# Moving all 128x128 transposes of an attention and MLP layer from TensorE to crossbar DMAs

## The chip, the cores and the metric

One core of a Trainium2 chip. The metric is the device time of one execution in microseconds (us). Runs of one kernel agree within about 0.7%. Engine names: PE is TensorE, PEld its weight load, DVE is VectorE, ACT is ScalarE, POOL is GpSimd, SP is SyncE. "SPq" and "ACTq" rows are DMA issues on the two rings.

## The reference

Tokens S = 2048, width D = 1024, 32 query heads of 32 with one shared K and V head, MLP width F = 3584, all bf16.

```python
h  = x + A(layernorm(x))        # A: q = x wq (32 heads), k = x wk, v = x wv,
                                #    softmax(q k^T / sqrt(32)) v, then wo
h2 = h + B(layernorm(h))        # B: (sigmoid(x w_gate) * (x w_up)) w_down
```

A matmul here contracts over the partitions, so three intermediates have to be transposed in 128x128 blocks: the normalised x (16 tiles of 128x1024), the attention output (16 tiles) and the normalised h (16 tiles).

## The kernel before

A planner in Python simulates the five engines with assumed durations and emits one fixed, in-order instruction list for each engine. Semaphores keep the result correct whatever the real times are. The order is the planner's guess.

Names used below: `xT` transposes the normalised x; `KV` makes K and V; `Q0` and `Q` make the queries; `S` is a block of scores, followed by two exponentials `Pr` on ACT; `PV` is the product with V; `OTt` transposes the attention output; `OP` is the output projection; `hT` transposes the second norm's result; `GU(c)` is the gate and up product of token chunk c (256 tokens, 28 groups); `D(c)` is the down product. GU(0) needs the attention of query tiles 0 and 1 (128 exponentials), their OP, the second norm and hT.

```python
# the planner's model of one DMA (all DMAs are on the SP ring)
if o.nbytes:
    go = max(s + 1300.0, self.dma_free)
    self.dma_free = go + o.nbytes / 260.0
    o.end = self.dma_free + 700.0
...
PRIO = ["xT", "KV", "Q0", "PV", "OTt", "OP", "hT", "D", "GU", "Q"]   # who fills TensorE first
...
def mk_xT(t):                                   # head: 8 TensorE transposes, one PSUM copy
    def atoms(b):
        tp = F_ps[:, b, :].bitcast(BF16)
        return [(lambda dt=dt: PE.transpose(out=tp[:, dt * P:(dt + 1) * P],
                 in_=xn[:, t % 2, dt * P:(dt + 1) * P], identity=ident[:, :]), P, []) for dt in range(DT)]
    def after(b, last):
        ...                                     # ACT or DVE copies PSUM to xnT, then the next norm is queued
...
def mk_OTt(hh):                                 # attention output: 4 transposes, DVE copy to OT (32 groups)
def mk_hT(t):                                   # second norm: 8 transposes, DVE copy to hnT (16 groups)
...
# when the last Q group is done: w_down, 7.3 MB in four pieces, into the memory of xnT and wq
for i in range(4):
    wd_ld.append(dma(lambda ...: SP.dma_start(wd_sb[:, a:b2, :], ...), f"wd{i}", 7 * P * D * 2, [last], prio=4))
```

All matmul groups except S share two PSUM banks (F_ps). A bank is free again when its copy has been made.

The softmax here doesn't subtract the row's maximum and nothing guards it: scores larger than these inputs give would overflow.

## Time and profile before

| | before |
|---|---|
| median time | 1221.6 us (3 runs; 1223.2 with the fourth, taken beside the change) |
| TensorE busy / ACT busy | 1174.0 / 1042.1 of 1223.8 us |
| first K/V matmul | 13.75 us |
| first exponential | 27.3 us |
| first GU(0) matmul | 177.7 us |

From the page of the kernel before: the busy times, then the rows of the 40 slices (digits are tenths of a slice of 30.6 us; PEclk is the granted TensorE clock in tenths).

```profile
PE 1174.0 (96%) x22016; PEld 835.1 (68%) x22016; DVE 316.4 (26%) x838; ACT 1042.1 (85%) x1283; POOL 47.2 (4%) x109
PE   4899979999999999999999999999999999999999
ACT  6899999999999999999999999999999989711120
PEclk9999989999999999999999999999999999999999
DMA  9411175562056601565016460256303653089390
```

TensorE and ACT are both full from the third slice on. The exponentials end near 1062 us, and the last 160 us are bound by TensorE. So TensorE work that disappears from the middle, or an idle TensorE that is filled, shortens the tail. The dip to 8 in slice 6 is a stretch where TensorE has too little to do.

The table of stretches, TensorE only: from:to, length, busy us (instructions), granted clock, DMA share, GB/s.

```profile
0.00:60.00 60.00, 38.86 (x705) 1.00 0.72 222
60.00:150.00 90.00, 89.32 (x1806) 1.00 0.13 38
150.00:210.00 60.00, 50.74 (x1132) 0.91 0.61 199
210.00:265.00 55.00, 54.56 (x1164) 1.00 0.58 157
265.00:1060.00 795.00, 780.97 (x15952) 1.00 0.39 109
```

TensorE idles 21.1 us in the first 60, 9.3 us in the stretch around 180 us, and 14.0 us in the long middle. Between 150 and 210 us the Q groups have been used up and GU(0) may not start yet: the attention alone, paced by ACT, leaves TensorE partly empty.

The TensorE timeline at two places in the middle, with start, length, and in brackets the idle time before with its releaser. First an OTt group, then the two hT groups of a chunk:

```profile
678.18 0.76 PE L330 MATMUL F_ps<-hnT,ring 128*128 128x256 bf16 x3
678.78 0.39 PE L558 MATMUL F_ps<-ident,Osb 128*128 128x128 bf16 x4
679.68 0.60 PE L330 MATMUL F_ps<-wo_sb,OT 128*128 128x512 bf16 x2 [0.52 <-DVE OT L566]
...
1019.93 0.61 PE L619 MATMUL F_ps<-ident,hn 128*128 128x128 bf16 x8
1020.47 0.40 PE L330 MATMUL S_ps<-QTb,kT 32*128 32x128 bf16 x16
1021.33 0.62 PE L619 MATMUL F_ps<-ident,hn 128*128 128x128 bf16 x8 [0.45 <-DVE hnT L625]
1021.78 1.03 PE L330 MATMUL F_ps<-zone,hact 128*128 128x512 bf16 x4
```

Four transposes stream in 0.23 us (eight start within 0.62 us, which is 57 ns each), but from the start of the OTt group to the next instruction 0.90 us pass, because the next group waits for the copy.

### The profile page before, as it was taken

The numbers are of one execution on the slowest core, as the hardware profiler recorded it, in microseconds if no ns is written. First come the engines' busy times: TensorE is split into PE (matmuls) and PEld (weight loads), VectorE is DVE, ScalarE is ACT, GpSimd is POOL, SyncE is SP. The second block draws the span as 40 slices with busy tenths as digits, with TensorE's granted clock in tenths as the row PEclk, the third lists the DMA queues.
The fourth block names the chain that finished last, engine by engine and source line by source line (L and its number), as shares of the span: only waits on it lengthen the run. The fifth ranks groups of instructions, "written<-read, shape, count | busy, mean of one in ns | idle before, by whom it ended". The sixth has DMA issues, their size and how long they took to land.

```text
span 1223.8 us, 47137 instructions
## 1 busy us (share of the span) xinstructions
PE 1174.0 (96%) x22016; PEld 835.1 (68%) x22016; DVE 316.4 (26%) x838; ACT 1042.1 (85%) x1283; POOL 47.2 (4%) x109
## 2 busy tenths in 40 slices
PE   4899979999999999999999999999999999999999
PEld 3665557785678756877568675778657776587684
DVE  8523321212222222223121222132222212232121
ACT  6899999999999999999999999999999989711120
POOL 6100000000000000000000000000000000000000
PEclk9999989999999999999999999999999999999999
DMA  9411175562056601565016460256303653089390
GB/s 320 116 28 41 42 260 156 148 173 64 20 149 174 192 20 46 150 191 148 16 50 191 119 170 20 70 165 184 111 20 86 172 148 102 15 224 263 105 252 18
DMA packets 258612, 151.02 MB, mean 123 GB/s; under 512 B 7280, under 2 KB 248944, under 8 KB 258416
## 3 DMA queue, kind: packets, MB, share of 16 engines
q1 hardware_dynamic: 258416, 148.00, 43.1%
q8 instruction: 173, 2.83, 1.0%
q14 instruction: 23, 0.19, 0.0%
HBM read 140.64 MB, written 7.34 MB: 121 GB/s over the span
## 4 chain that ended last, share of the span: by engine, by line
PE 63%; ACT 31%; issue 3%; DVE 2%; POOL 0%; DMA 0%
PE F_ps L330 54%; ACT Pr L495 28%; PE S_ps L330 9%; ACT tnh L669 1%; ACT zone L313 1%; PE F_ps L619 0%; ACT zone L230 0%; DVE OT L566 0%; DVE st L274 0%; DVE st L276 0%; PE F_ps L558 0%; DMA ring<-in_A_x_dram 0%; POOL dsb L287 0%; DVE hnT L625 0%; DVE ring L307 0%
## 5 line engine op out<-in xcount | busy, mean ns | idle before, releaser
L495 ACT ACTIVATE Pr<-S_ps 128x1024 bf16<-128x1024 f32 x1024 | 972.4, 1052 | 26.4 <-PE S_ps L330 25.9
L330 PE MATMUL F_ps<-hnT,ring 128*128 128x256 bf16 x3584 | 440.6, 275 | 2.5 <-DVE OT L566 1.2
L330 PEld LDWEIGHTS F_ps<-hnT,ring 128*128 128x128 bf16 x3584 | 332.5, 98 | 61.3 <-issue 3.1
L330 PEld LDWEIGHTS F_ps<-Vaug,Pr 128*128 128x128 bf16 x8192 | 229.7, 96 | 28.1 <-issue 4.1
L330 PE MATMUL F_ps<-Vaug,Pr 128*128 128x33 bf16 x8192 | 244.4, 178 | 2.4 <-issue 1.5
L330 PE MATMUL S_ps<-QTb,kT 32*128 32x128 bf16 x8192 | 208.5, 218 | 15.4 <-ACT Pr L495 10.1
L330 PE MATMUL F_ps<-zone,hact 128*128 128x512 bf16 x896 | 213.2, 380 | 0.8 <-DVE OT L566 0.5
L330 PEld LDWEIGHTS S_ps<-QTb,kT 32*128 32x128 bf16 x8192 | 119.2, 93 | 127.9 <-ACT Pr L495 81.6
L676 DVE SCALAR_TENSOR_TENSOR hact<-tnh,F_ps 128x256 bf16<-128x256 f32 x224 | 94.3, 421 | 384.0 <-ACT tnh L669 383.9
L669 ACT ACTIVATE tnh<-F_ps 128x256 f32<-128x256 f32 x224 | 90.7, 405 | 115.0 <-PE F_ps L330 115.0
L330 PEld LDWEIGHTS F_ps<-zone,hact 128*128 128x128 bf16 x896 | 79.2, 98 | 91.3 <-DVE OT L566 0.7
L330 PE MATMUL F_ps<-zone 128*128 128x256 bf16 (+2 forms) x512 | 76.5, 292 | 3.1 <-POOL rstd L290 1.2
L707 DVE SCALAR_TENSOR_TENSOR h_sb<-F_ps,h_sb 128x512 bf16<-128x512 f32 x32 | 22.1, 692 | 203.1 <-PE F_ps L330 203.1
L330 PE MATMUL F_ps<-wo_sb,OT 128*128 128x512 bf16 x256 | 64.2, 381 | 3.8 <-DVE OT L566 3.7
L531 DVE RECIPROCAL rL<-F_ps 128x4 f32<-128x4 f32 x128 | 23.4, 183 | 133.7 <-PE F_ps L330 133.5
L330 PEld LDWEIGHTS F_ps<-zone 128*128 128x128 bf16 x512 | 37.5, 98 | 24.2 <-ACT zone L230 1.4
L284 POOL TENSOR_SCALAR zb<-mvb 128x1 bf16<-128x1 bf16 x32 | 7.5, 233 | 1026.4 <-DVE mvb L280 1026.1
L330 PEld LDWEIGHTS F_ps<-wo_sb,OT 128*128 128x128 bf16 x256 | 21.0, 97 | 28.4 <-DVE OT L566 6.9
L533 DVE TENSOR_TENSOR Osb<-F_ps,rL 128x128 bf16<-128x128 f32 x128 | 37.2, 291 | 3.8
L594 DVE TENSOR_TENSOR h_sb<-F_ps,xres 128x512 bf16<-128x512 f32 x32 | 22.1, 692 | 54.4 <-PE F_ps L330 54.4
L337 PE MATMUL F_ps<-ident,zone 128*128 128x128 bf16 x128 | 11.0, 236 | 17.3 <-POOL dsb L287 9.1
L231 DVE CAST hact<-F_ps 128x512 bf16<-128x512 f32 x24 | 16.6, 692 | 40.2 <-PE F_ps L330 40.2
(39 smaller groups left out, 232.4 us busy)
## 6 DMA issues: line engine op xcount, KB each, us to landing
ring<-in_B_w_gate_dram SPq DMA_DIRECT2D x112, 512.0 KB, 4.1
ring<-in_B_w_up_dram SPq DMA_DIRECT2D x112, 512.0 KB, 5.9
zone<-in_B_w_down_dram SPq DMA_DIRECT2D x4, 1792.0 KB, 15.4
ring<-in_A_x_dram SPq DMA_DIRECT2D x16, 256.0 KB, 7.0
xres<-in_A_x_dram SPq DMA_DIRECT2D x16, 256.0 KB, 2.7
out_dram<-h_sb SPq DMA_DIRECT2D x32, 128.0 KB, 1.7
q_scratch<-hact SPq DMA_DIRECT2D x24, 128.0 KB, 1.8
QTb<-q_scratch SPq DMA_DIRECT2D x6, 512.0 KB, 6.3
```

What stands on the lines that cost most here:

```text
L231: lambda: DVE.tensor_copy(out=out_ap, in_=in_ap))
L284: f = pl.op("pool", lambda: POOL.tensor_scalar(out=zb[:, ph, t:t + 1], in0=mvb[:, ph, t, 1:2], scalar1=LN_EPS_BF16, scalar2=None, op0=ALU. ...
L313: xnorm[t] = evac(lambda: ACT.activation(out=dst, in_=src, func=ACTF.Copy, scale=sc), lambda: DVE.tensor_scalar(out=dst, in0=src, scalar1= ...
L330: return lambda: PE.matmul(o, lhsT=l, rhs=r, start=start, stop=stop, **kw)
L337: return [(lambda dt=dt: PE.transpose(out=tp[:, dt * P:(dt + 1) * P], in_=xn[:, t % 2, dt * P:(dt + 1) * P], identity=ident[:, :]), P, []) ...
L495: exps[u] = pl.op("act", lambda slot=slot, pb=pb: ACT.activation(out=Pr[:, slot, :].rearrange("p (a b) -> p a b", a=2), in_=S_ps[:, pb:pb ...
L531: a = pl.op("dve", lambda: DVE.reciprocal(rL[:, k, :].unsqueeze(2), ov[:, :, DH:DH + 1]), [last], prio=0, occ=70, lat=280)
L533: e = pl.op("dve", lambda: DVE.tensor_tensor(out=Osb[:, hh % 2, (g % 4) * P:(g % 4 + 1) * P].rearrange("p (a b) -> p a b", a=4), in0=ov[:, ...
L594: h_ev[(t, dc)] = pl.op("dve", lambda: DVE.tensor_tensor(out=h_sb[:, t % 4, sl], in0=F_ps[:, b, :], in1=xres[:, t % 2, sl], op=ALU.add), [ ...
L669: a = pl.op("act", lambda: ACT.activation(out=tnh[:, k, :], in_=F_ps[:, b, 0:256], func=ACTF.Tanh, scale=0.5), [last, tn_user.get(k)], pri ...
L676: e = pl.op("dve", lambda: DVE.scalar_tensor_tensor(out=hactT[:, ft, :], in0=tnh[:, k, :], scalar=1.0, in1=F_ps[:, b, 256:512], op0=ALU.ad ...
L707: e = pl.op("dve", lambda: DVE.scalar_tensor_tensor(out=h_sb[:, t % 4, sl], in0=F_ps[:, b, :], scalar=0.5, in1=h_sb[:, t % 4, sl], op0=ALU ...
```

## The change

The intent: take 384 transposes and their PSUM copies off TensorE, DVE and ACT; put them on DMAs that transpose in the crossbar. The transposes go on the SP ring, so the loads of the head move to the ACT ring. The first norm is made in place, and its small operations are batched for pairs of tiles; the planner also gets new assumed durations for the statistics of both norms.

```diff
@@ planner
-        self.dma_free = 0.0
+        self.dma_free = collections.Counter()          # one per ring
...
-            go = max(s + 1300.0, self.dma_free)
+            go = max(s + 1300.0, self.dma_free[e])
@@ head
-            x_ld[t] = dma(lambda: SP.dma_start(...), f"x{t}", P * D * 2, prio=0)
+            x_ld[t] = dma(lambda: ACT.dma_start(...), f"x{t}", P * D * 2, prio=0, ring="act")
   (wk, wv, wq and wo likewise: 21 loads on the ACT ring)
+                if t < 1 or t >= 10:
+                    xnorm[t] = pl.op("dve", ... multiply x_sb by rstd in place ...)
+                else:
+                    xnorm[t] = pl.op("act", ... the same on ACT ...)
+                xT_ev[t] = dma(lambda t=t: SP.dma_start_transpose(
+                    out=xnT[:, :, t * P:(t + 1) * P], in_=x_sb[:, t, :]), f"xT{t}", P * D * 2, [xnorm[t]], prio=0)
@@ attention output: mk_OTt is gone
+                    ot_ev[qb] = dma(lambda: SP.dma_start_transpose(out=OT[:, qb % 4, :, :], in_=Osb[:, qb % 2, :]), ...)
@@ second norm: mk_hT is gone
+                hT_ev[t] = dma(lambda t=t: SP.dma_start_transpose(
+                    out=hnT[:, :, (t % 2) * P:(t % 2 + 1) * P], in_=hn[:, t % 2, :]), ...)
```

(cut to its core)

## The prediction

> **What bounds the kernel now.** By the busy table PE is busy 1174.0 of 1223.8 us and ACT 1042.1. From 60 to 1060 us both are full: the table of stretches gives, for 265 to 400 us, PE 133.1 and ACT 132.0 of 135. The PE timeline there shows a score block (16 matmuls) every 1.86 us, which is two exponentials at 0.93 us: ACT paces the attention, and PE fills the time between with PV, output projection and MLP matmuls. What does not fit is left to a tail without exponentials, from about 1062 us on (GU(6), then D 24.3, GU 49.1, D 24.3 us): pure TensorE. So TensorE work taken out of the middle should come off the tail, nearly one for one. ACT time alone is worth little.
>
> **What is removed.**
> - 384 PE transposes. Eight start within 0.62 us, so about 57 ns each: 256 in the middle (attention output, second norm) = 14.6 us, 128 in the head = 7.3 us.
> - PE waits for their PSUM copies: the list of waits gives PE <- OT copy 5.5 us and PE <- hnT copy 1.2 us, of which perhaps 4 us go for good; 64 fewer users of the two PSUM banks.
> - The copies: DVE OT 13.5, DVE hnT 11.1, ACT xT 11.3, DVE xT 3.4 us. DVE is 26% busy, so this counts only in the head.
>
> **What is added.** 48 crossbar DMAs of 256 KB on the SP ring. This trace has none. The Trainium skill, "VectorE: DVE Perf Modes", section "The three transpose paths", gives 1309 ns for one 128x128 block, and "DMA: Bandwidth & Descriptors", section "Latency and other measured facts", 261 GB/s. Estimate from both: 1.3 + 0.9 us, plus generating and queueing, 3 to 5 us to landing (a plain 256 KB load lands in 2.7 us). The kernel's static plan assumes 3.0 us. PE executes a fixed order: if a transpose lands later than planned by more than the placement slack (about 1 us, half a matmul group), PE stalls in front of the output projection, 16 times, and each stall also delays the next scores. The second-norm transposes hide behind D (24 us).
>
> **Head.** 21 loads move to the ACT ring. On SP their issue lasted until 14.7 us (timeline)[...]; now ACT, which must scale tiles 1 to 9, is held instead. First K/V matmul: about 19 to 21 us (was 13.75). Afterwards PE has no transposes and no copy waits (it idled 19 of the first 40 us) and should be full from about 22 us. DVE still needs about 35 us for statistics, so the last tile lands at about 42 us, as before. Net gain 3 to 6 us.
>
> **Sum.** 14.6 + 4 + 4.5 = 23 us gained; expected stalls before the output projection about 4 us (0.25 us each if landing takes 4 us, 1 us each at 5, 3 us each at 7). Predicted 1202 us, range 1183 to 1235. Chances: faster by over 2% 0.42, within 2% 0.43, slower 0.15.
>
> **What would show it.** Transposes land in 3 to 5 us; PE waits for the OT DMA under 10 us in all; PE busy down by about 30 us in the table; the last exponential within 12 us of 1062, and the tail after it shorter by 10 us or more; the first K/V matmul near 20 us; the exponential still 0.93 us apart.
>
> **What would make it wrong.** Crossbar transposes of 8 us or more, or stuck behind 1 MB of weight loads in the same ring: PE stalls of 5 us times 16 would make it 5% slower. Transposes disturbing the weight loads, of which the tail wants 1 MB per 3.5 us. Or a head much better than reckoned, as ACT and PE both get freer.

## The result

The changed kernel took 1212.2 us (median of 4 runs, 1211.99 to 1213.17). A ratio here is the mean time of one kernel's fast runs over that of the kernel before in the same rounds, so not quite the ratio of the medians quoted. The ratio is 0.991, with a 95% interval of 0.9885 to 0.9934: about 11 us faster, which is less than 2%.

The same lines of the page, after:

```profile
PE 1148.6 (95%) x21632; PEld 812.1 (67%) x21632; DVE 287.8 (24%) x762; ACT 1037.1 (86%) x1281; POOL 39.4 (3%) x86
PE   0899957999999999999999999999999999999999
ACT  1679998999999999999999999999999999991120
PEclk9999957999999999999999999999999999999999
DMA  9941271666146541657236660576326750569390
```

TensorE has 25 us less busy time, but it starts a whole slice later, and slices 6 and 7 show a thin TensorE at a clock of 5 to 7 tenths. The attention now ends near 1086 us, and the tail after it is shorter.

The table of stretches after, columns as before:

```profile
0.00:60.00 60.00, 24.27 (x324) 1.00 0.97 254
60.00:150.00 90.00, 88.45 (x1725) 1.00 0.29 70
150.00:210.00 60.00, 40.02 (x1009) 0.66 0.46 149
210.00:265.00 55.00, 55.00 (x1151) 1.00 0.61 165
265.00:1060.00 795.00, 793.81 (x15991) 1.00 0.49 126
```

Idle TensorE before 265 us grew from 31.5 us (21.1 + 0.7 + 9.3 + 0.4) to 57.3 us (35.7 + 1.6 + 20.0 + 0.0). In the long middle it fell from 14.0 to 1.2 us. The change did its work in the middle and lost much of it in the head.

What held up the head. Rows of the changed kernel's timelines: TensorE's first matmul, then ACT, then DVE.

```profile
30.52 8.02 PE L335 MATMUL F_ps<-zone 128*128 128x256 bf16 x72 [30.52 <-DMA zone<-ring]
...
15.38 0.47 ACTq L260 DMA_DIRECT2D wo_sb<-in_A_wo_dram  x1
15.95 1.28 ACT L319 ACT_TABLE_LOAD   x1 [15.95 <-issue]
17.24 3.23 ACT L319 ACTIVATE ring<-ring,rstd 128x1024 bf16<-128x1024 bf16 x3
32.85 0.39 ACT L228 ACTIVATE kT<-F_ps 128x256 bf16<-128x256 f32 x1 [12.39 <-PE F_ps L335]
...
50.77 0.42 DVE L229 CAST QTb<-F_ps 128x256 bf16<-128x256 f32 x1 [15.39 <-PE F_ps L335]
```

Three things are to be seen. ACT issued loads until 15.9 us and scaled tile 1 only then, done at 18.4 us. TensorE's first K/V matmul then waited for a crossbar DMA until 30.5 us. And because TensorE was late, ACT and DVE each stood 12 and 15 us at an eviction of a TensorE result, in front of norms that were ready to be worked on.

The crossbar DMAs' own record, "to landing", which is the time from issue to arrival (minimum, median, maximum) for x, then the attention output, then the second norm:

```profile
DMA to landing us min/median/max: 3.2/4.7/12.5
...
DMA to landing us min/median/max: 3.0/3.6/7.3
...
DMA to landing us min/median/max: 3.0/3.5/4.8
```

The view of one tile's instructions, for the exponentials and for GU, before and then after; "first and last start" are the numbers to read.

```profile
L495 ACT ACTIVATE Pr<-S_ps x1024: 1017/1045/1205, 27.3 to 1060.6; 128x1024 bf16<-128x1024 f32 x171
L330 PE MATMUL F_ps<-hnT,ring x3584: 269/273/421, 177.7 to 1196.5; 128*128 128x256 bf16 x200
```

```profile
L478 ACT ACTIVATE Pr<-S_ps x1024: 1017/1030/1142, 41.6 to 1084.9; 128x1024 bf16<-128x1024 f32 x171
L335 PE MATMUL F_ps<-hnT,ring x3584: 269/273/421, 202.9 to 1182.8; 128*128 128x256 bf16 x200
```

The exponentials begin 14 us later, and GU(0) begins 25 us later. In the first 100 us, 64 exponentials had started before and 44 after.

### The profile page after: what moved, and what is told of

The parts are those of the page before. It is cut to its first block, busy times and chain, and to the rows that moved or that the text cites. A ratio compares the mean times of both kernels' runs of the same rounds, so it can differ in the third digit from the quotient of the medians.

```text
span 1210.2 us, 46354 instructions
## 1 busy us (share of the span) xinstructions
PE 1148.6 (95%) x21632; PEld 812.1 (67%) x21632; DVE 287.8 (24%) x762; ACT 1037.1 (86%) x1281; POOL 39.4 (3%) x86
## 4 chain that ended last, share of the span: by engine, by line
PE 86%; ACT 10%; DMA 2%; ACTq 1%; issue 0%; DVE 0%
PE F_ps L335 73%; PE S_ps L335 13%; ACT Pr L478 9%; DMA zone<-ring 2%; ACTq L238 1%; ACT ring L319 1%; ACTq L249 0%; ACT QTb L228 0%; ACTq L244 0%; DVE h_sb L659 0%; ACT kT L228 0%; ACTq L260 0%; ACTq L242 0%; ACT Vaug L228 0%; ACT L319 0%
## 5 line engine op out<-in xcount | busy, mean ns | idle before, releaser
L335 PE MATMUL S_ps<-QTb,kT 32*128 32x128 bf16 x8192 | 210.4, 220 | 18.7 <-ACT Pr L478 17.5
L620 ACT ACTIVATE tnh<-F_ps 128x256 f32<-128x256 f32 x224 | 88.1, 393 | 82.3 <-PE F_ps L335 82.3
L335 PE MATMUL F_ps<-zone 128*128 128x512 bf16 (+2 forms) x512 | 76.7, 297 | 36.7 <-DMA zone<-ring 34.7
L288 POOL TENSOR_SCALAR zb<-mvb 128x1 bf16<-128x1 bf16 (+1 forms) x25 | 5.6, 223 | 1060.1 <-DVE mvb L284 1059.9
L335 PEld LDWEIGHTS F_ps<-wo_sb,OT 128*128 128x128 bf16 x256 | 21.8, 98 | 23.5 <-issue 2.4
L228 ACT ACTIVATE kT<-F_ps 128x256 bf16<-128x256 f32 x7 | 2.8, 393 | 18.1 <-PE F_ps L335 18.1
```

The lines of the kernel that those rows point to most:

```text
L288: f = pl.op("pool", lambda: POOL.tensor_scalar(out=zb[:, ph, sl].unsqueeze(2), in0=mvb[:, ph, sl, 1:2], scalar1=LN_EPS_BF16, scalar2=None, ...
L335: return lambda: PE.matmul(o, lhsT=l, rhs=r, start=start, stop=stop, **kw)
L620: a = pl.op("act", lambda: ACT.activation(out=tnh[:, k, :], in_=F_ps[:, b, 0:256], func=ACTF.Tanh, scale=0.5), [last, tn_user.get(k)], pri ...
```

## The experiments

Twelve kernels, all correct, three calls, each call on its own chip with its own runs of the kernel before (medians 1223.9, 1222.1 and 1225.6 us). Ratios are against those. The kernel before differs by up to 3.5 us between calls, so a difference of a few us between kernels of different calls is weak.

| kernel | median us | ratio (95%) | first K/V, us | exponentials begun by 100 us | GU(0) at, us |
|---|---|---|---|---|---|
| before | 1221.6 | 1 | 13.8 | 64 | 177.7 |
| changed | 1212.2 | 0.991 (0.9885 to 0.9934) | 30.5 | 44 | 202.9 |
| mid_only | 1200.1 | 0.9794 (0.9766 to 0.9822) | 13.4 | 66 | 197.3 |
| head_only | 1239.0 | 1.0111 (1.0082 to 1.0140) | 30.3 | 43 | 199.4 |
| wo_late | 1211.8 | 0.9891 (0.9862 to 0.9920) | 26.5 | 43 | 204.5 |
| dve_first | 1212.8 | 0.9894 (0.9859 to 0.9928) | 25.1 | 43 | 203.9 |
| mid_wd | 1197.7 | 0.9785 (0.9748 to 0.9822) | 13.6 | 65 | 183.9 |
| after_wd | 1214.0 | 0.9935 (0.9901 to 0.9968) | 30.0 | 45 | 201.9 |
| before_wd | 1222.3 | 0.9996 (0.9960 to 1.0031) | 13.9 | 64 | 177.7 |
| head_fix | 1211.7 | 0.9912 (0.9882 to 0.9942) | 25.7 | 47 | 200.5 |
| after_plan | 1207.9 | 0.9859 (0.9844 to 0.9874) | 30.6 | 57 | 205.2 |
| head_fix_plan | 1207.3 | 0.9850 (0.9832 to 0.9868) | 23.5 | 60 | 202.4 |
| mid_OT | 1209.6 | 0.9876 (0.9859 to 0.9893) | 13.4 | 66 | 194.8 |
| mid_hT | 1209.2 | 0.9868 (0.9852 to 0.9883) | 13.6 | 65 | 184.9 |

### First call: the two halves apart, and two causes of the late head

**mid_only**: the head of the kernel before, the middle of the change. (All four kernels that have only a part of the change keep its new planner durations for the statistics.)

```diff
  (against the changed kernel)
-  first norm in place, start_transpose of x on SP, loads on the ACT ring, pairs of tiles
+  mk_xT with TensorE transposes and PSUM copies, loads on the SP ring, as before
```

> The kernel before with only the middle of the change: attention output and second norm are transposed by crossbar DMAs, the head (first norm, its transposes on TensorE, loads on the SP ring) as before. Theory A (the middle gains about 30 us, the late head gives about 18 us back): first K/V matmul near 14 us, first exponential near 27 us, stretch with a lowered TensorE clock no longer than before's (about 30 us at 0.83 to 0.86), time 1185 to 1195 us. Rival B (the head is harmless, the long stretch at half clock after 150 us comes with the transposing DMAs or with the w_down load as such): clock 0.5 for 40 us again, time 1205 to 1215 us. Rival C (the middle is worth only what was predicted for it, 15 to 19 us, and the head is neutral to slightly bad): 1203 to 1208 us.

Measured: 1200.1 us, ratio 0.9794. The first K/V matmul and the first exponential (27.3 us) are where they were before. The time lies between A and C, above the range of A by 5 us. B falls on the time, which is 12 us below the changed kernel's, though the clock still goes to half: for 34 us after 150 us, against 41 us in the changed kernel and 10 us before. But A had said that the low clock would be no longer than before's, and that is wrong, as is its silence on GU(0), which starts at 197.3 us, 20 us later than before.

**head_only**: the head of the change, with OTt and hT on TensorE.

```diff
  (against the changed kernel)
-  ot_ev[qb] = dma(... start_transpose OT ...);  hT_ev[t] = dma(... start_transpose hnT ...)
+  mk_OTt(hh) and mk_hT(t) with TensorE transposes and DVE copies, as before
```

> The kernel before with only the head of the change: first norm in place, its 16 transposes on crossbar DMAs, loads on the ACT ring, small operations paired; attention output and second norm transposed on TensorE as before. Theory A: first K/V matmul near 30 us, first exponential near 41 us, GU(0) 20 to 25 us later than in the kernel before, time 1235 to 1245 us. Rivals B and C: within 8 us of the kernel before, 1215 to 1230 us.

Measured: 1239.0 us, ratio 1.0111, so about 14 us slower than before. A holds, B and C fall. The two halves multiply to 0.9794 x 1.0111 = 0.9903, and the whole change measured 0.991. So the change is a gain of about 25 us in the middle and a loss of about 14 us in the head. The half clock is here too, for 34 us after 150 us, with no transposing DMA after 67 us; so it does not come with these DMAs as such.

**wo_late**: does the load traffic delay the transposes?

```diff
-        wo_ld = dma(lambda: ACT.dma_start(wo_sb ...), "wo", D * D * 2, prio=1, ring="act")
+        wo_ld = dma(lambda: SP.dma_start(wo_sb ...), "wo", D * D * 2, [xT_ev[NT - 1]], prio=1)
```

> The changed kernel, with the 2 MB load of wo taken off the ACT ring and put on the SP ring behind the last crossbar transpose of x. If the transposes of x land late because they share the DMA engines with the queued loads (theory A1), their issue and landing get shorter and the first K/V matmul moves from 30.5 us to 24 to 27 us, time 1204 to 1209 us. If they are late because ACT scales x1 late after issuing 21 loads (A2), the matmul stays at 29.5 to 30.5 us and the time at 1211 to 1213 us.

Measured: the first K/V matmul moved from 30.5 to 26.5 us, as A1 says. The time did not move (1211.8 us), and A1's time is wrong.

**dve_first**: does ACT's issue work delay tile 1?

```diff
-                if t < 1 or t >= 10:
+                if t < 4 or t >= 10:
```

> The changed kernel, with tiles 1 to 3 scaled on DVE and not on ACT (so not behind the issue of 21 loads and the table load). A2 (ACT's issue work delays x1): x1 is ready at about 12 us and not at 18.4, the first K/V matmul moves to 22 to 25 us, time 1203 to 1208 us. A1 (the loads hold up the transposes until they have drained): the transposes are issued earlier but land late all the same, the first K/V matmul is at 27 us or later, time 1208 to 1213 us.

Measured: the first K/V matmul moved to 25.1 us, near A2's 22 to 25 us, so ACT's issue work is a part too. Again the time did not move (1212.8 us), and the second K/V group still waited for a transpose until 33 us.

Both causes of the late start are real, worth 4 to 5 us each at the first matmul. Neither shows a gain in the end, and both kernels had 43 exponentials begun by 100 us, as many as head_only. An early start alone was not what counted.

### Second call: the w_down load, and the head with its queues cleared

In mid_only, the DMA issues on SP between 148 and 195 us read so (start, issue time):

```profile
148.89 8.49 SPq L426 DMA_DIRECT2D zone<-in_B_w_down_dram  x4
157.42 5.38 SPq L420 DMA_DIRECT2D q_scratch<-hact  x1
162.84 5.10 SPq L542 DMA_TRANSPOSE OT<-Osb  x1
...
194.00 1.39 SPq L602 DMA_TRANSPOSE hnT<-hn  x1
```

The second OT transpose is issued behind 7.3 MB of w_down; its landing took 10.4 us, the longest of the 16. The projection that needs it began at 181.3 us, and in the kernel before at 164.2 us.

**mid_wd**: mid_only with w_down in 14 pieces during GU(0).

```diff
-                    for i in range(4): ... wd_ld.append(dma(... 7 * P * D * 2, [last], prio=4))   # after the last Q group
+                if c == 0 and ft < 14:                                                             # in GU(0), one per group
+                    wd_ld.append(dma(... wd_sb[:, 2*ft:2*ft+2, :] ..., 2 * P * D * 2, [last], prio=4))
```

> The kernel with only the middle of the change (1200.1 us), with the 7.3 MB load of w_down cut into 14 pieces that are issued during GU(0), so that no transpose queues behind it. Theory D (the second attention transpose waits behind w_down in the SP ring, in the plan and on the chip, which moved its output projection from 164 to 181 us and GU(0) from 177.6 to 197.3 us): the transpose lands in 3 to 4 us instead of 10.4, the projection starts by 170 us, GU(0) by 182 us, the stretch at half clock shrinks to at most 25 us, time 1185 to 1194 us. Rival (GU(0) is late for another reason, such as the clock, and w_down is harmless): GU(0) stays near 197 us, time 1197 to 1202 us.

Measured: the transpose was issued at 162.1 us, the projection began at 166.0, GU(0) at 183.9 us. So theory D is right about the wait. The time is 1197.7 us, ratio 0.9785 against 0.9794: their intervals overlap, so no gain is shown, and the expected 1185 to 1194 us is missed. The table of stretches of mid_only (first two lines) and of mid_wd shows where the gain went:

```profile
150.00:210.00 60.00, 42.07 (x1056) 0.72 0.51 162
210.00:265.00 55.00, 54.88 (x1125) 1.00 0.64 169
```

```profile
150.00:210.00 60.00, 46.46 (x1037) 0.77 0.44 122
210.00:265.00 55.00, 51.98 (x1039) 0.97 0.91 246
```

Idle TensorE fell by 4.4 us in the first stretch and rose by 2.9 us in the second, where the pieces of w_down and GU's own weights now share the DMA engines (share 0.91). (Both traces lack 91 matmul records, the same number in these stretches, so the differences stand.) The third OT transpose now landed after 7.4 us and not 3.3, and its projection began at 257.0 us and not 232.1. So a wait seems moved rather than removed; the profile gives no releaser for most of the new idle time.

**after_wd**: the same edit on the changed kernel.

> The changed kernel (1212.2 us) with w_down cut into pieces during GU(0). In it the second attention transpose is issued at 182 us, after w_down has drained at about 177 us, because its attention runs late from the head. Theory D with a late head: nothing to win before GU(0), which stays at 198 to 204 us; time 1206 to 1213 us. Rival (w_down costs the changed kernel itself, by contention): GU(0) by 190 us and time below 1204 us.

Measured: 1214.0 us, GU(0) at 201.9 us: nothing to win, as theory D says for a late head (the time is 1 us above the range). In the changed kernel the attention itself is late, and its second OT transpose is issued at 182 us, when w_down has landed (at 172.4 us).

**before_wd**: the control, the same edit on the kernel before.

> Control: the kernel before with w_down cut into pieces during GU(0). It has no crossbar transposes to queue behind w_down, so by theory D nothing changes by more than 4 us: 1218 to 1226 us, GU(0) at 174 to 179 us. If w_down's burst in itself starved TensorE: below 1214 us.

Measured: 1222.3 us, GU(0) at 177.7 us, as expected. Without crossbar transposes, nothing queues behind w_down that matters.

**head_fix**: the changed kernel with three queues of the head cleared.

```diff
   (wo_late, and:)
-                if t < 1 or t >= 10:
+                if t < 16 or t >= 10:                      # every tile scaled on DVE
-            load_slab(s, [xT_ev[k] for k in range(4 * s, 4 * s + 4)])
+            load_slab(s, [xT_ev[k] for k in range(NT)])    # prefetch after the last transpose
```

> The changed kernel with three causes of the late head removed together: wo loaded behind the last transpose of x, all 16 tiles scaled on DVE (none on ACT behind the issue of 21 loads or behind an eviction that waits for TensorE), and the weight-slab prefetch only after all 16 transposes. If the slow head comes from these queues: last x transpose issued by 48 us (61.4 in the changed kernel), first K/V matmul by 25 us, at least 58 exponentials in the first 100 us (46 in the changed kernel, 67 before), time 1199 to 1206 us. If crossbar transposes are slow in the head by themselves, next to any loads: last transpose at 55 us or later, under 52 exponentials, time 1208 to 1213 us.

Measured: 1211.7 us, 47 exponentials by 100 us, first K/V matmul at 25.7 us, last transpose issued at about 57 us. (Counted by starts, the 46 and 67 exponentials of the expectation are 44 and 64.) Both theories as I had put them are wrong in part. The transposes were quick once the loads had drained (about 1.3 us apart, median landing 3.3 us), so they are not slow by themselves. Yet the last one was late. Its releaser shows why: SP waited 14.0 us in one piece for a query eviction on DVE, behind which the norm of tiles 14 and 15 stood in the list. It is the same kind of wait as the 15.39 us shown for the changed kernel. The lists had been ordered by a planner that expected TensorE to deliver much sooner.

### Third call: the planner's order, and the middle's two parts

**after_plan**: the changed kernel; only the planner's model is different.

```diff
-            go = max(s + 1300.0, self.dma_free[e])
-            self.dma_free[e] = go + o.nbytes / 260.0
-            o.end = self.dma_free[e] + 700.0
+            go = max(s + 1300.0, self.dma_free["all"])
+            self.dma_free["all"] = go + o.nbytes / 260.0
+            o.end = self.dma_free["all"] + 700.0
```

> The changed kernel; only the planner is told that both rings share one DMA bandwidth (one counter in place of one per ring), so that it expects the transposes of x late and orders DVE and ACT for that. Theory E (the in-order lists do the greater part of the head's harm: DVE stood 15 us at an eviction of a late TensorE group with the last tiles' norm queued behind it, ACT 12 us likewise): those waits go, the last transpose of x is issued by 50 us (61.4 in the changed kernel), 55 or more exponentials in the first 100 us (44 by the same count), GU(0) before 195 us, time 1200 to 1207 us. Rival (the late start of TensorE at 30 us is itself the harm, whatever the order): first K/V matmul still near 30 us, 44 to 50 exponentials, time 1210 to 1214 us.

Measured: 1207.9 us, ratio 0.9859 against 0.991 for the changed kernel (in another call, intervals apart). DVE's wait for query groups in the list of waits (total us, times, longest us), in the changed kernel and then here:

```profile
DVE QTb L229 <- PE F_ps L335: 16.7, 4, 15.4
```

```profile
DVE QTb L229 <- PE F_ps L335: 11.5, 15, 1.7
```

The first K/V matmul is as late as ever (30.6 us), the longest wait of DVE for a query group is 1.7 us in place of 15.4, the last transpose is issued at 45.7 us in place of 61.4, and 57 exponentials have begun by 100 us in place of 44. So the order did matter: 4 us by the medians, 6 us by the ratios, of the head's 14 came back with not one engine doing different work. The rival falls; what holds back the rest was not isolated. But GU(0) is at 205 us, not before 195, and the time is just above the range. The SP issues of this kernel say why: with the attention earlier, its second OT transpose is now the one behind w_down.

```profile
156.45 8.95 SPq L403 DMA_DIRECT2D zone<-in_B_w_down_dram  x4
165.44 5.11 SPq L397 DMA_DIRECT2D q_scratch<-hact  x1
170.60 5.72 SPq L519 DMA_TRANSPOSE OT<-Osb  x1
```

**head_fix_plan**: head_fix with the same planner edit.

> The version with wo and the slab prefetch late and all tiles scaled on DVE (1211.7 us, first K/V matmul 25.7 us, last x transpose issued at about 57 us), with the planner's shared DMA counter as well. Theory E: the 14 us wait of DVE at a query eviction goes, the last transpose is issued by 46 us, 60 or more exponentials in the first 100 us, time 1197 to 1204 us, level with the kernel that keeps the head on TensorE (1200.1). Rival: no better than 1208 us.

Measured: the first K/V matmul at 23.5 us, the last transpose issued at 45.7 us, 60 exponentials by 100 us: the wait is gone as theory E says. The time of 1207.3 us is 3 us above its range; the ratio 0.985 is the same as after_plan's within the intervals. GU(0) at 202.4 us has the same queue before it (second OT transpose issued at 167.8 us, right behind w_down). With w_down moved as well it might do better; this was not run.

**mid_OT** and **mid_hT**: mid_only with only one of the two kinds on DMAs.

```diff
  mid_OT:  hT back on TensorE (mk_hT as before)
  mid_hT:  OT back on TensorE (mk_OTt as before)
```

> The kernel before with only the attention-output transposes on crossbar DMAs (second norm's and the head's on TensorE). In the kernel before, the time from the start of such a group on TensorE to its next instruction sums to 18.7 us over 32 groups (7.3 us of it streaming). Expected 10 to 17 us faster than before: 1206 to 1213 us. If only the streaming counts: 1215 to 1218 us.

> The kernel before with only the second norm's transposes on crossbar DMAs (attention output and head on TensorE). The same sum over its 16 groups is 10.7 us (7.3 us of it streaming). Expected 7 to 11 us faster than before: 1211 to 1216 us; this and the attention-output part should add up to the 23 us of both within 5 us.

Measured: ratios 0.9876 and 0.9868 of 1225.6 us, so about 15 and 16 us faster each. For the attention output that fits the 18.7 us of TensorE time that its groups held (starts to next starts, summed in the trace of before), of which only 7.3 us is streaming. For the second norm 16 us is more than the 10.7 us counted, and its time is 2 us below the range. The parts add up to 31 us, and both together gave about 25: outside the 5 us that I had allowed, though the three intervals together (about 2, 2 and 3.4 us to each side) leave little of the 6 us certain. In mid_OT and mid_only GU(0) is late behind w_down (194.8 and 197.3 us), in mid_hT less (184.9 us). But mid_wd, which removed that wait, did not bring the 6 us back. The traces say where mid_hT's time went. Summed over all TensorE instructions, each from its start to the next start, its own groups gave 10.7 us, GU 3.2 us (414.6 to 411.4), the score blocks 3.0 us (190.7 to 187.7) and the head's own transposes 1.5 us (19.1 to 17.6). The last is in mid_OT as well (17.5) and so is counted twice; the planner durations that both keep from the change are a likely reason, but no run has them alone. Why GU and the score blocks wait less, and why the two parts do not add, stays open.

## Why the prediction was right or wrong

The time (1212.2 us) lies in the range of 1183 to 1235 us, 10 us above the figure of 1202. But that is partly luck: the range is wide enough to hold the kernel before as well, and the figure contains two larger errors that partly cancel, about 10 us too little gain in the middle and about 18 us too much in the head.

- **What bounds the kernel**: right. ACT paces the middle, TensorE fills it, and what TensorE saves there shortens the tail: the middle alone was worth 25 us.
- **The middle, 14.6 + 4 - 4 us**: too small. The terms that were mis-sized are what the groups hold beyond streaming ("waits for their PSUM copies", put at 4 us) and the stalls. The list of waits showed 6.7 us, but it counts only what the modelled ends leave open; by starts, from each of the 48 transpose groups to the next instruction, 29.4 us passed (18.7 + 10.7), 14.6 of it streaming. Only part of the other 14.8 us is waiting for copies (about 7 us in 10 OTt groups); the rest is score blocks that waited for an exponential, about 0.1 us at each change to a score block, and smaller waits. The stalls expected before the output projection (4 us) did not show: TensorE's list of waits has no entry for the OT transposes, whose median landing was 3.6 us, within the expected 3 to 5.
- **The head, a gain of 3 to 6 us**: wrong in sign; it lost about 14 us (head_only). The step that failed is "First K/V matmul: about 19 to 21 us" with "should be full from about 22 us". ACT's held-up scaling was foreseen, and tile 1 was ready at 18.4 us. What I had not applied to the head was the danger that I named at the end, transposes stuck behind loads. The Trainium skill, "DMA: Bandwidth & Descriptors", section "Issuing engines are not separate DMA queues", says that DMAs of all issuers run on the same 16 DMA engines and interleave. The trace agrees: from 10 to 30 us the engines moved 358 GB/s, 6.6 of 7.2 MB of it for the ACT ring's loads, and the second transpose, on the other ring, landed only 11.9 us after its tile was scaled, when one in the middle takes 3.0 (least) to 3.6 us (median). With 2 MB of loads out of the way (wo_late) it took 8.2 us; issued 6.6 us earlier into the same loads (dve_first), 13.1 us.
- **The predicted signs**: the last exponential within 12 us of 1062: wrong, it started at 1084.9. The tail shorter by 10 us or more: right (from about 162 to 124 us, from the end of the last exponential to the end of the span). TensorE busy down by about 30 us: 25.4. An exponential still 0.93 us apart: right in kind, the median spacing in the middle is 0.92 us in both.
- **"The last tile lands at about 42 us, as before"**: wrong, its transpose was issued at 61.4 us. Nothing in the prediction asked what the fixed lists do when a planned time is missed. One late DMA made TensorE late, a late TensorE held DVE and ACT at evictions, and these held the next norms. after_plan shows this chain by removing it.

A count by starts, which needs no modelled ends, puts the two traces side by side: TensorE's first start, and then the time from each start to the next. From before to the change, the first start came 21.4 us later (9.1 to 30.5 us), the score blocks took 7.9 us more and the projections 5.9 us more, and 48.5 us of transposes went, 19.1 of them in the head. The other groups differ by 0.5 us at most; the sum is the 13.6 us between the two spans. So the late start alone cost more than the head's transposes had held.

How much of the loss is due to the half clock between 156 and 190 us was not measured. It stands beside a TensorE that is busy for 5 to 7 of each 10 us, and all its idle times of over 1 us there ended with an exponential on ACT.

The best versions that were run are mid_only (1200.1 us, ratio 0.9794) and mid_wd (1197.7 us, 0.9785): the change in the middle, TensorE in the head. They beat both kernels (the intervals against the kernel before include the 2% mark); between them no difference is shown.

## What to carry to other kernels

Move a transpose to a DMA where the DMA engines have room and something else fills the latency (here the middle, DMA share 0.49: 25 us gained); try leaving it on TensorE where loads fill the engines and the result is wanted at once (here the head, share 0.95 in head_only: 14 us lost). Where the instruction order is fixed ahead of time, a wrong latency in the plan has a cost of its own (4 to 6 us here), because other engines' lists wait in line; give the planner one shared DMA bandwidth, not one for each ring. And measure a TensorE group by the time from its start to the next start, which its busy time and the list of waits do not show in full; then look what the next instruction waited for, since only some of these groups held TensorE until their PSUM copy was made.

## What the Trainium skill lacked or had wrong

- "Advanced Engine Details and Errata", section "X-Bar Transpose (TRN2)", calls transposing DMAs as fast as regular ones. Here a 256 KB transpose from SBUF to SBUF landed in 3.0 us at best and 3.5 to 3.6 us in the median of the middle, against a median of 2.6 us for a 256 KB load of xres. That is near, with the DMA engines about half busy (share 0.49). The section says nothing of how late a transpose lands next to heavy loads: 12.5 us at worst in the changed kernel's head (share 0.97), 16.7 us in dve_first's.
- "VectorE: DVE Perf Modes", section "The three transpose paths", gives one figure for one 128x128 block on the DMA path (1309 ns). Eight blocks in one DMA landed in 3.0 us, about 0.4 us a block; the figure must not be multiplied. For TensorE it gives 390 ns a block; back to back they started 57 ns apart here, and from the first start of a group to the next instruction 29.4 us passed in 48 groups, 14.6 of it streaming.
- No page gives by name for this chip how long SP's sequencer is occupied by issuing such a transpose (there are only cycle counts for "previous generations" in a part on another chip): at least 1.23 us each here, against 0.34 us for a plain load of the same size.
- "TensorE: Matmul & The Clock Gate", section "What's actually happening", gives the low clock to a TensorE that was idle for a window of about 3.4 us. Here the granted clock stood at 0.5 from 156 to 190 us while TensorE's longest gap in the timeline from 150 us on was 1.43 us; it was busy for 5 to 7 of each 10 us. A later section of the page, "A second HAM failure mode: psum-queue depth-cycling", does tell of a kernel whose frequent short idle times made the clock swing; neither gives the share of busy time at which that happens.
